# A fused linear attention and gated feed-forward kernel: another written order, full 128-row chunks of k, and a swap of two products

## The chip, the cores and the metric

The kernel runs on one core of one Trainium2 chip. The metric is device time in microseconds (us) of one execution; three runs of the kernel before gave 933.54, 933.70 and 934.96 us, median 933.7 us. The engines are called as the profile calls them: PE (TensorE, the matrix engine), DVE (VectorE), ACT (ScalarE), POOL (GpSimd) and SP (SyncE, which here only issues DMAs).

## The reference

Inputs q, k, v are 8 batches x 8 heads x 576 rows x 64, in float32; the attention output is laid out as x with 4608 tokens x 512 and goes through a gated feed-forward of width 1536.

```
q_s = softmax(q, over the 64 columns);  k_s = softmax(k, over the 576 rows)
kv  = einsum('bhsd,bhse->bhde', k_s, v)
x   = einsum('bhsd,bhde->bhse', q_s, kv)           # -> 4608 x 512
xn  = x / sqrt(mean(x * x, -1) + 1e-6) * rms_g
g   = xn @ w_gate;  val = xn @ w_val
out = (g / (1 + exp(-g)) * val) @ w_out
```

A softmax over the rows of k subtracts each column's maximum, takes the exponential and divides by the sum over the 576 rows; a row with exponential 0 adds nothing to either sum.

## The kernel before

**Tiles and stages.** The 4608 tokens are cut into nine blocks j = 0 to 8 of 512. The 8 heads are four pairs g = 0 to 3. For each batch b and pair g the kernel loads k twice (`kt` by rows, `kd` transposed), takes the column maxima from `kd` (`k_max`, DVE), spreads them over the partitions on PE (`k_rows`), subtracts (`k_sub`), takes exponentials (`k_exp`, ACT) and multiplies with v on PE (`k_mm`, L600). The 576 rows are five chunks: four of 128 and one of 64, two heads each, so `k_mm` is ten matmuls and each stands in the trace as two instructions. For batches 1 to 7 `k_seg` puts the `k_mm` of one pair and the `k_rows` of the next in one bank of PSUM. `kv_hi` and `kv_lo` scale the product and split it into a high and a low word.

**q.** For block j and pair g, `q_load` to `q_mul` make the softmax of q, `q_t` transposes, `q_hi` and `q_lo` split into words, and `q_x` (L796) sums three products on PE for each batch that the block touches: high kv with high q, low kv with high q, high kv with low q. Block 0 and 1 have their own forms (`q_load0` to `q_x0`), and batch 0 transposes k on PE (`k_tr0`).

**Feed-forward.** Weights arrive as 64-bit floats in 36 tiles of 512 KB (`load_w`) in staging slots and are turned into float32 by ACT and DVE or POOL (`conv_low`, `conv_mul`, `conv_one`, `conv_shift`, `conv_sign`). Block 0 uses float32 words (`f1`, L1230; `f2`, L1301), block 1 16-bit words (`f1p`, L1246), blocks 2 to 8 a scheme of seven products per pair of slices instead of eight (`pp`, L1166) with its copies and sums (`ev`), the split of h (`hu_hi`, `hu_lo`) and the output product (`fu`, L1214). `store` scales and writes the output.

**Order.** Nothing is scheduled at build time: the string `ORDER` (some 3,000 steps) is run from first to last, and each engine executes what its steps issue in that order, from its own queue. A suffix `:A`, `:D` or `:P` names the engine (ACT, DVE, POOL) of a step that could run on several. An instruction that waits holds up all that stands behind it on its engine. SP issues all loads and stores in one queue: a load whose tile is still in use holds up every later load.

**Dummy work.** `warm` (L470) multiplies constants before the first product, and `fill` (L476) adds products with zero to an open sum; neither changes a result. `zeros` is the common part:

```
def zeros(t, n, fresh):
    for _ in range(n):
        nc.tensor.matmul(t, lhsT=zero_b..., rhs=ones_b..., start=fresh, stop=fresh)
```

In `ORDER`, `fill.20` is twenty such matmuls at that place. The listing follows with the profile's line numbers.

Of the kernel before, what the change touches and what calls it, by code (L numbers as in the profile page):

```python
# [29 lines left out]
q_exp.0.0 v_load.0.2 q_max0.0.2 q_sum0.0.0 load_w.0.1 q_sub0.0.1:P fill.2 k_mm.0.0 q_exp.0.3 k_rec.0.2 q_sum0.0.3  # L30
kv_norm0.0.0:A q_sub0.0.2:P load_w.1.1 q_exp.0.1 g_abs q_eps0.0.0 q_exp.0.2 q_rec0.0.0 q_sum0.0.1 v_load.0.1
q_mul0.0.0:P conv_low.0.0.1 kd_load.1.0 k_max.0.1 conv_mul.0.0 fill.12 q_t0.0.0 q_eps0.0.3 k_exp.0.1 conv_shift.0.0
load_w.3.0 k_tr0.2.0 conv_sign.0.0 q_c0.0.0:A k_tr0.2.1 k_ev0.2.0:A q_rec0.0.3 fill.2 q_x0.0.0 load_w.2.2 q_eps0.0.1
q_rec0.0.1 q_mul0.0.3:P k_ev0.2.1:A q_sum0.0.2 load_w.1.2 q_mul0.0.1:P conv_low.3.2.1 k_tr0.3.0 x_hi.0.0:D x_sq.0.0
load_w.2.1 x_lo.0.0 k_tr0.3.1 k_ev0.3.0:A k_mm.0.2 q_eps0.0.2 k_ev0.3.1:A q_load0.1.0 q_rec0.0.2 conv_low.0.1.1
k_eps.0.1 k_rec.0.1 q_mul0.0.2:P conv_mul.0.1 k_mm.0.3 k_load.1.0 conv_low.1.0.2 k_eps.0.3 k_rec.0.3 conv_shift.0.1
k_tr0.1.0 v_load.1.0 kv_norm0.0.3:A k_tr0.1.1 conv_sign.0.1 n_sum0.0 v_load.1.1 kv_norm0.0.2:A k_max.1.0 w_hi.0.0.2:P
q_t0.0.3 conv_mul.1.0 q_t0.0.1 q_c0.0.3:D load_w.4.1 conv_low.3.0.2 conv_shift.1.0 q_x0.0.3 q_c0.0.1:A conv_sign.1.0
w_lo.0.0:P f1.0.0.0.0 x_sq.0.3 f1.0.1.0.0 x_hi.0.3:D s_tr k_ev0.1.0:A kd_load.1.1 x_lo.0.3 w_lo.0.1:P k_ev0.1.1:A
fill.3 k_mm.0.1 conv_low.2.2.1 s_top load_w.0.2 conv_low.1.2.1 s_rows s_bits kv_norm0.0.1:A load_w.4.0 k_rows.1.0  # L40
conv_low.2.0.2 q_x0.0.1 k_load.1.1 q_max0.1.0 q_t0.0.2 x_sq.0.1 x_hi.0.1:D q_load0.1.1 q_sub0.1.0:P q_c0.0.2:A
n_sum0.1 x_lo.0.1 q_load0.1.2 v_ones.1.0 q_exp.1.0 q_x0.0.2 k_sub.1.0 k_load.1.2 v_ones.1.1 f1.0.1.0.1 q_sum0.1.0
conv_mul.1.1 f1.0.1.0.3 f1.0.0.0.1 load_w.5.0 f1.0.0.0.3 x_hi.0.2:D x_sq.0.2 k_exp.1.0 conv_shift.1.1 fill.1 n_sum0.2
conv_sign.1.1 f1.0.1.0.2 f1.0.0.0.2 conv_low.0.2.1 f1.0.0.1.0 x_lo.0.2 f1.0.1.1.0 w_hi.1.0.2:P load_w.5.1 f1.0.1.1.1
conv_mul.0.2 f1.0.0.1.1 k_max.1.1 n_sum0.3 conv_low.4.0.2 conv_shift.0.2 kd_load.1.2 f1.0.0.1.2 f1.0.0.1.3 f1.0.1.1.2
conv_sign.0.2 f1.0.0.2.0 f1.0.1.1.3 w_lo.1.1:P f1.0.1.2.0 f1.0.1.2.1 n_t.0 conv_mul.2.0 load_w.4.2 f1.0.1.2.2
f1.0.0.2.1 f1.0.0.2.2 n_y0.0 conv_one.2.0 w_lo.1.0:P f1.1.0 conv_shift.2.0 n_y1.0 conv_mul.2.1 conv_sign.2.0:P
load_w.6.0 conv_low.5.0.2 f1.0.1.2.3 conv_shift.2.1 f1.0.0.2.3 k_mm.1.0 conv_sign.2.1 f1.1.1 v_load.1.2 n_cols.0
w_hi.2.0.2:A load_w.6.1 k_load.1.3 k_max.1.2 conv_low.4.2.1 w_lo.2.0:P q_max0.1.1 kd_load.1.3 conv_mul.1.2 n_rows.0
q_sub0.1.1:P g_mul.0 conv_shift.1.2 f1.2.0 w_lo.2.1:P silu.0 conv_sign.1.2 conv_low.6.0.2 v_ones.1.2 h_mul.0  # L50
load_w.5.2 conv_mul.3.0 q_eps0.1.0 g_mul.1 f1.2.1 conv_shift.3.0 silu.1 conv_sign.3.0 g_mul.2 conv_mul.3.1 load_w.7.0
q_max0.1.2 conv_one.3.1 silu.2 conv_shift.3.1 q_sub0.1.2:P conv_low.5.2.1 q_rec0.1.0 k_rows.1.1 k_eps.1.0 k_rec.1.0
conv_sign.3.1:P h_mul.2 kv_norm0.1.0:A h_mul.1 conv_mul.3.2 w_hi.3.0.2:P load_w.7.1 k_max.1.3 f2.0 conv_shift.3.2
kd_load.2.0 q_exp.1.2 conv_sign.3.2 q_exp.1.1 w_lo.3.0:P k_sub.1.1 load_w.7.2 conv_mul.2.2 q_sum0.1.1 conv_mul.4.0
q_mul0.1.0:P conv_shift.2.2 conv_low.7.0.2 conv_sign.2.2 w_lo.3.1:P q_load0.1.3 k_exp.1.1 conv_shift.4.0 load_w.6.2
conv_mul.4.1 q_eps0.1.1 q_rec0.1.1 conv_mul.4.2 conv_shift.4.1 q_mul0.1.1:P conv_low.7.2.1 f1.3.0 conv_sign.4.1
conv_one.4.0 q_load.2.0 conv_shift.4.2 conv_mul.5.2 conv_sign.4.0:P load_w.8.1 conv_sign.4.2 conv_low.6.2.1
conv_shift.5.2 conv_mul.5.0 load_w.8.2 w_hi.4.0.2:P f2.1 load_w.8.0 o_hi.4:A g_mul.3 conv_shift.5.0 conv_sign.5.0
o_lo.4:P silu.3 conv_sign.5.2 load_w.10.0 conv_mul.5.1 q_max0.1.3 load_w.10.2 fill.20 q_t0.1.0 conv_one.5.1 w_lo.4.1:P
f2.2 conv_shift.5.1 conv_low.8.2.1 q_c0.1.0:D conv_low.8.0.2 q_sub0.1.3:P q_max.2.0 conv_mul.6.0 conv_sign.5.1:P  # L60
q_sum0.1.2 conv_mul.6.1 conv_shift.6.0 conv_one.6.0 w_lo.4.0:P load_w.10.1 f1.3.1 conv_shift.6.1 conv_mul.6.2
conv_low.10.2.1 conv_sign.6.1 conv_sign.6.0:P o_hi.5:A conv_shift.6.2 conv_mul.7.0 o_lo.5:P conv_sign.6.2 f1.4.0
w_hi.5.0.2:A conv_shift.7.0 conv_mul.7.1 conv_sign.7.0 w_lo.5.1:P conv_one.7.1 conv_shift.7.1 load_w.9.0 conv_mul.7.2
w_lo.5.0:P h_mul.3 q_x0.1.0 conv_low.10.0.2 conv_shift.7.2 f1.4.1 conv_sign.7.1:P x_sq.1.0 conv_sign.7.2 x_raw.1.0:A
g_mul.4 load_w.9.2 conv_mul.8.0 load_w.9.1 q_eps0.1.2 q_rec0.1.2 q_half.2.0 conv_mul.8.1 q_mul0.1.2:P f2.3
w_hi.6.0.2:A conv_shift.8.0 q_load.2.1 conv_shift.8.1 conv_mul.8.2 w_lo.6.1:P conv_sign.8.1 silu.4 conv_low.9.2.1
conv_shift.8.2 load_w.11.1 w_lo.6.0:P conv_mul.9.0 h_mul.4 warm.2.13 conv_low.9.0.2 conv_sign.8.2 f1.5.0 h_hi.4:P
q_max.2.1 conv_one.8.0 load_w.11.2 h_lo.4:P conv_shift.9.0 conv_mul.9.1 conv_one.9.1 conv_sign.9.0 conv_sign.8.0:P
f1.6.0 g_mul.5 conv_mul.9.2 conv_shift.9.1 silu.5 load_w.11.0 conv_low.11.2.1 conv_sign.9.1:D conv_mul.10.0
conv_shift.9.2 f2.4 conv_one.10.0 conv_shift.10.0 conv_sign.9.2 conv_mul.10.1 conv_sign.10.0:P g_mul.6 n_sq.0.0  # L70
conv_shift.10.1 k_mm.1.1 o_hi.6:P silu.6 conv_sign.10.1 n_sq.0.1 f1.5.1 v_load.1.3 k_eps.1.1 o_lo.6:P k_rec.1.1
k_load.2.0 kv_norm0.1.1:D conv_mul.11.0 conv_mul.11.1 conv_low.11.0.2 f1.6.1 h_mul.5 w_hi.7.0.2:P conv_one.11.1
conv_shift.11.0 h_hi.5:A conv_shift.11.1 conv_sign.11.0 conv_mul.10.2 w_lo.7.0:P f1.7.0 w_hi.8.0.2:A h_mul.6
conv_shift.10.2 conv_sign.11.1:P conv_mul.11.2 conv_sign.10.2 h_hi.6:A w_lo.8.0:P conv_shift.11.2 k_rows.1.2 k_sub.1.2
w_lo.8.1:P q_exp.1.3 g_mul.7 fill.5 n_col.0.0 k_exp.1.2 n_max.0.0 w_lo.7.1:P f1.7.1 conv_sign.11.2 n_sq.0.2 q_sum0.1.3
v_ones.1.3 h_lo.5:P n_sq.1.0 n_col.0.1 w_hi.9.0.2:A h_lo.6:P k_mm.1.2 n_max.0.1 k_rows.1.3 n_sq.1.1 k_eps.1.2
v_load.2.0 f1.8.0 k_rec.1.2 w_lo.9.1:P k_sub.1.3 k_load.2.1 kv_norm0.1.2:A k_exp.1.3 n_bits.0.1.0 q_eps0.1.3
q_rec0.1.3 w_lo.9.0:P k_mm.1.3 g_mul.8 q_mul0.1.3:P silu.7 q_t0.1.1 k_eps.1.3 k_rec.1.3 f1.8.1 silu.8 q_c0.1.1:D
kv_norm0.1.3:A h_mul.7 n_bits.0.1.1 n_bits.0.1.2 n_bits.0.1.5 w_sc.0.1 n_bits.0.1.3 n_bits.0.1.4 q_x0.1.1 h_mul.8
w_hi.10.0.2:P b_hi.0.2:A n_col.1.0 w_sc.0.0 k_max.2.0 f1.9.0 n_max.1.0 kd_load.2.1 x_sq.1.1 x_raw.1.1:D b_lo.0.2:P  # L80
b_hi.0.3:A b_hi.0.0:A x_acc.1.1:D n_sq.1.2 n_col.1.1 f1.9.1 b_lo.0.0:D v_ones.2.0 k_load.2.2 n_sq.2.2 n_max.1.1
w_lo.10.0:P g_mul.9 n_sq.2.0 b_lo.0.3:D q_t0.1.2 q_max2.2.0 w_lo.10.1:D n_sq.2.1 q_load.2.2 n_col.2.0 f2.5 t_op.0.0:D
silu.9 n_max.2.0 w_hi.11.0.2:P n_sq.3.0 h_mul.9 q_c0.1.2:D b_hi.0.1:A t_hi.0.0:A q_t0.1.3 b_lo.0.1:D n_col.2.1
# [1299 lines left out]
```

## Time and profile before

| | |
|---|---|
| three runs | 933.54, 933.70, 934.96 us |
| the profiled execution | span 930.9 us; the runs' median is 2.8 us above it |
| PE busy | 913.8 us (98%), 6479 matmuls |
| DVE, ACT, POOL busy | 617.3, 559.1, 305.9 us |
| matmuls of L1166 (`pp`) on the chain that ended last | 38% of the span |
| matmuls of L1214 (`fu`) on it | 22% |
| bytes moved | 68.06 MB, 365 GB/s over the first 39 us |

How to read it: the span runs from the first to the last instruction of the program. "Busy" counts time in which at least one instruction of an engine is under way; a matmul's end is modelled, so a wait shorter than its pipeline does not show as idle time. The name `<-` points from what is read to what is written, and "idle before, releaser" names what ended the engine's last wait.

### The profile page before, as it was taken

Reading aid. Unit: us, or ns where it says so; the run is one execution under the profiler, and the core shown is the slowest. Engines: PE = TensorE matmul, PEld = TensorE weight load, DVE = VectorE, ACT = ScalarE, POOL = GpSimd, SP = SyncE. Lnnn points to the kernel's source line nnn. Section 1 sums busy time; section 2 is a strip of 40 time slices with the busy share of each in tenths; the row PEclk is TensorE's granted clock in tenths of the full one; section 3 lists DMA queues with packets and bytes.
Section 4 is the critical chain, followed back from the end, with each engine's and each line's share of the span. In section 5 each row is a group of like instructions: output and inputs, shape, how many; then the busy total and the mean of one; then the engine's idle time right before and its main releaser. Section 6 shows DMA issues by size and latency. Waiting matters only on the chain.

```text
span 930.9 us, 16383 instructions
## 1 busy us (share of the span) xinstructions
PE 913.8 (98%) x6479; PEld 644.0 (69%) x6479; DVE 617.3 (66%) x1330; ACT 559.1 (60%) x880; POOL 305.9 (33%) x304
## 2 busy tenths in 40 slices
...
GB/s 342 360 265 226 61 53 38 36 23 188 54 53 131 33 42 24 110 94 53 66 117 77 65 53 29 36 51 1 38 35 23 1 2 46 1 1 24 23 1 46
DMA packets 29550, 68.06 MB, mean 73 GB/s; under 512 B 3744, under 2 KB 4000, under 8 KB 29472
## 3 DMA queue, kind: packets, MB, share of 16 engines
...
q8 instruction: 51, 0.84, 0.4%
...
## 4 chain that ended last, share of the span: by engine, by line
PE 83%; DVE 6%; ACT 4%; DMA 3%; issue 2%; POOL 1%; SPq 0%; ACTq 0%; POOLq 0%; DVEq 0%
PE ps_gv L1166 38%; PE ps_o L1214 22%; PE ps_o L1301 5%; PE ps_gv L1230 5%; PE ps_gv L1246 4%; PE ps_a L796 2%; PE ps_a L600 2%; DMA qt<-in_q_dram 1%; PE ps_a L560 1%; DMA w_gv<-in_kt_dram 1%; DMA w_br<-in_w_dram 1%; PE ps_a L1021 1%; ACT w_gv L388 0%; PE ps_a L725 0%; DVE x_raw L827 0%
## 5 line engine op out<-in xcount | busy, mean ns | idle before, releaser
L1166 PEld LDWEIGHTS <-w_gv 128*128 128x128 f16 x2016 | 196.0, 98 | 39.7 <-issue 3.2
L1166 PE MATMUL ps_gv<-xo,w_gv 128*128 128x256 f16 x1296 | 155.8, 273 | 0.6 <-ACT w_br L383 0.4
L1166 PE MATMUL ps_gv<-x_op,w_gv 128*128 128x256 f16 x720 | 86.5, 273 | 0.2
L1166 PEld LDWEIGHTS <-w_br 128*128 128x128 f16 x756 | 73.7, 98 | 14.3 <-issue 1.3
L1214 PEld LDWEIGHTS <-hh 128*128 128x128 f16 x504 | 48.9, 98 | 49.8 <-issue 0.4
L1214 PEld LDWEIGHTS <-hl 128*128 128x128 f16 x504 | 49.0, 98 | 47.5 <-issue 0.6
L1214 PE MATMUL ps_o<-w_o,hl 128*128 128x512 f16 x336 | 79.9, 379 | 0.0
L1214 PE MATMUL ps_o<-w_o,hh 128*128 128x512 f16 x336 | 78.4, 379 | 0.0
L1230 PE MATMUL ps_gv<-xo,wf 128*128 128x512 f32 x264 | 66.7, 404 | 0.0
L1166 PE MATMUL ps_gv<-xo,w_br 128*128 128x256 f16 x540 | 66.1, 273 | 0.0
L1230 PEld LDWEIGHTS ps_gv<-xo,wf 128*128 128x128 f32 x264 | 49.0, 188 | 12.9 <-issue 2.8
L1166 PEld LDWEIGHTS <-wf 128*128 128x128 f16 x504 | 49.2, 98 | 8.1 <-issue 0.3
L1181 DVE TENSOR_TENSOR tm<-ps_gv,tm 128x512 f32<-128x512 f32 x29 | 20.0, 689 | 50.9 <-PE ps_gv L1166 47.7
L785 POOL TENSOR_TENSOR ql<-qT,qh 128x512 fp32r<-128x512 f32 x14 | 18.2, 1301 | 87.1 <-ACT qh L383 87.1
L383 ACT COPY ps_gv<-ps_gv 128x512 f32<-128x512 f32 x42 | 24.0, 572 | 36.3 <-PE ps_gv L1166 13.8
L1181 DVE TENSOR_TENSOR w_br<-ps_gv,w_br 128x512 f32<-128x512 f32 x29 | 20.0, 690 | 37.4 <-PE ps_gv L1166 36.8
L1166 PE MATMUL ps_gv<-xo,wf 128*128 128x256 f16 x360 | 43.9, 273 | 0.0
L897 POOL TENSOR_TENSOR acc<-acc,sq 128x512 f32<-128x512 f32 x11 | 14.0, 1270 | 71.8 <-ACT sq L893 71.8
L1246 PE MATMUL ps_gv<-x_op,w_br 128*128 128x512 f16 x144 | 31.9, 379 | 0.0
L383 ACT COPY w_br<-ps_gv 128x512 f32<-128x512 f32 x29 | 17.0, 585 | 23.5 <-PE ps_gv L1166 23.4
L970 POOL TENSOR_TENSOR wf<-w_gv,wf 128x512 fp32r<-128x512 f32 x22 | 28.1, 1293 | 6.7 <-ACT wf L383 6.3
L383 ACT COPY tm<-ps_gv 128x512 f32<-128x512 f32 x29 | 17.0, 585 | 21.5 <-PE ps_gv L1166 21.3
...
## 6 DMA issues: line engine op xcount, KB each, us to landing
...
```

What stands on the lines that cost most here:

```text
L383: (e.copy if e is nc.scalar else e.tensor_copy)(dst, src)
L600: nc.tensor.matmul(ps[h * D:(h + 1) * D, :n1], lhsT=ke[:n, h, j], rhs=vt_[b, g][:n, j, h], start=(j == 0), stop=(j == len(rows) - 1))
L785: on(nc.gpsimd).tensor_tensor(out=ql, in0=qT_[j, g], in1=qh_[j, g][0].bitcast(F32), op=ALU.subtract)
L796: nc.tensor.matmul(px[:, c0:c1], lhsT=wt, rhs=mv[:, c0:c1], start=(i == 0), stop=(i == 2))
L897: on(nc.gpsimd).tensor_tensor(out=acc_[j], in0=acc_[j], in1=sq_[j, g], op=ALU.add)
L970: on(nc.gpsimd).tensor_tensor(out=cut(wl[:, a]), in0=W(s, a), in1=cut(wh[:, a].bitcast(F32)), op=ALU.subtract)
L1166: nc.tensor.matmul(pair(ps, i), lhsT=a[:, wt], rhs=y if i else y.rearrange("p (a c) -> p a c", a=2), start=(first and k == 0 and i == 0 an ...
L1181: nc.vector.tensor_tensor(out=v, in0=bank[j, u, 5 if n == 5 else 3], in1=v, op=ALU.add)
L1214: nc.tensor.matmul(po[2 * n + t], lhsT=a[:, o:o + P], rhs=w, start=(u == 0 and i == 0 and p == 0), stop=(u == NU - 1 and i == 1 and p == 2))
L1230: nc.tensor.matmul(pd[s], lhsT=m[:, a, c * P:(c + 1) * P], rhs=X[j, c][x], start=(n == 1), stop=(n == 3 * NKT))
L1246: nc.tensor.matmul(pd[s], lhsT=w[:, wt], rhs=x, start=(c == 0 and p == 0), stop=(c == NKT - 1 and p == 2))
L1301: nc.tensor.matmul(po[t], lhsT=a[:, t * P:(t + 1) * P], rhs=w, start=(i == 0 and n == 0), stop=(i == NF - 1 and n == len(terms) - 1))
```

## The change

Three things change, and one name follows from them.

- `ORDER` is another sequence of the same steps, with other engines behind many of them; of 53 dummy matmuls of `fill`, 2 are left, and the 37 of `warm` stand elsewhere. Two of its lines:

```
-kd_load.0.0 exp_table constants kd_load.0.3 warm.9 kv_zero0.0 kd_load.0.2 kv_zero.2 q_load0.0.0 kv_zero0.1 q_load0.0.1
+constants warm.2.3 warm.2.12 warm.2.0 warm.2.7 warm.9 warm.2.5 kv_zero0.0 kd_load.0.2 k_max.0.2 k_exp.0.2 kd_load.0.0
```

- In batches 1 to 7 the host fills the last 64 rows of the fifth chunk of k with -1e30 in place of a repeat of the last row, and `k_mm` multiplies all 128 rows of every chunk.

```
-        rows = [min(P, S - c * P) for c in range(C0)]
+        rows = [P if b else min(P, S - c * P) for c in range(C0)]
...
-        "k": pairs(k)[1:, :, :, chunks].transpose(0, 1, 3, 2, 4, 5).reshape(b - 1, g, 128, -1),
+        "k": np.where(past, np.float32(-1e30), pairs(k)[1:, :, :, chunks]).transpose(0, 1, 3, 2, 4, 5).reshape(b - 1, g, 128, -1),
```

- In `q_x` the second and the third product change places.

```
-            for i, (wt, mv) in enumerate(((hi, qh), (lo, qh), (hi, ql))):
+            for i, (wt, mv) in enumerate(((hi, qh), (hi, ql), (lo, qh))):
```

- The output banks are kept under (block, number), `po[j, t]`, since a block's stores may now stand behind the next block's first output product.

Counted over the two instruction lists, PE issues 51 matmuls fewer, all of `fill`; ACT 87 instructions fewer, 12 loads of its function table more than before (76 instead of 64) among them; DVE 30 more and POOL 69 more; the DMAs are the same 204 rows in another order. `ORDER` is one line shorter, so line numbers below it are one less.

**The place where block 0's first `f1` products start, on PE.** Before, from the `k_mm` of batch 0, pair 1 on (L600); x is what `f1` multiplies, `wf` its weights, `tm` the squares for the norm:

```order
L600 MATMUL ps_o<-w_gv 64x64 x10
L994 MATMUL ps_a<-tp,ones 128x1
L560 MATMUL ps_a<-ident,kx 128x128
L725 MATMUL ps_o<-x_raw,ot 128x512
L712 MATMUL ps_o<-ident,x_op_94 128x128 x4
L914 MATMUL ps_a<-tm,mean_w 128x512
L725 MATMUL ps_o<-x_raw,ot 128x512
L1230 MATMUL ps_gv<-xo,wf 128x512 x4
L476 LDWEIGHTS zero_b
L476 MATMUL ps_gv<-ones_b,zero_b 128x512
L914 MATMUL ps_a<-tm,mean_w 128x512
L1230 MATMUL ps_gv<-xo,wf 128x512 x6
```

Now, from the same `k_mm` (L599) on:

```order
L599 MATMUL ps_o<-w_gv 64x64 x10
L724 MATMUL ps_o<-x_raw,ot 128x512 x2
L469 MATMUL ps_gv<-mean_w 128x512 x2
L987 MATMUL ps_a<-ident,mx 1x128
L469 MATMUL ps_gv<-mean_w 128x512 x2
L913 MATMUL ps_a<-tm,mean_w 128x512
L993 MATMUL ps_a<-tp,ones 128x1
L913 MATMUL ps_a<-tm,mean_w 128x512
L559 MATMUL ps_a<-ident,kx 128x128
L1229 MATMUL ps_gv<-xo,wf 128x512 x2
L913 MATMUL ps_a<-sq,mean_w 128x512
L1229 MATMUL ps_gv<-xo,wf 128x512 x15
```

All four transposes of q (L711) and all four `q_x0` (L724) now stand ahead of the first `f1`, where two `f1` products stood between them before; the `fill` is gone.

**The loads of k and v for batch 1, on SP.** `kt` is k by rows, `kd` k transposed, `vt` v, `qt` q; `w_br`, `w_gv` and `w_o` are staging slots of weight tiles. Before:

```order
L518 DMA kt<-in_k_dram 128x640
L680 DMA qt<-in_q_dram 128x512 x2
L518 DMA kt<-in_k_dram 128x640
L425 DMA w_br<-in_w_dram 128x1024 x2
L526 DMA kd<-in_kt_dram 128x576
L425 DMA w_br<-in_w_dram 128x1024
L425 DMA w_gv<-in_w_dram 128x1024
L541 DMA vt<-in_v_dram 128x650
L425 DMA w_gv<-in_w_dram 128x1024
L518 DMA kt<-in_k_dram 128x640
```

Now, with the last eight weight tiles:

```order
L424 DMA w_br<-in_w_dram 128x1024
L424 DMA w_gv<-in_w_dram 128x1024 x2
L424 DMA w_o<-in_w_dram 128x1024
L424 DMA w_br<-in_w_dram 128x1024 x2
L517 DMA kt<-in_k_dram 128x640
L424 DMA w_br<-in_w_dram 128x1024
L517 DMA kt<-in_k_dram 128x640
L424 DMA w_br<-in_w_dram 128x1024
L517 DMA kt<-in_k_dram 128x640
```

The rows of k for pairs 2 and 3 of batch 1 stood behind 14 and 19 of the 36 weight tiles, and now stand behind 36 and 34 of them (the last and the first `kt` of the second piece; the one between is of batch 2).

**One `q_x`, on PE.** Block 3, pair 0; `kv_hi_108` and `kv_lo_109` are the two words of kv of one batch, `kv` those of the other, `qh` and `ql` the words of q. Before:

```order
L796 MATMUL ps_a<-qh,kv_hi_108 128x256
L796 MATMUL ps_a<-qh,kv_lo_109 128x256
L796 MATMUL ps_a<-ql,kv_hi_108 128x256
L796 MATMUL ps_a<-qh,kv 128x320 x2
L796 MATMUL ps_a<-ql,kv 128x320
```

Now, the same `q_x`:

```order
L795 MATMUL ps_a<-qh,kv_hi_108 128x256
L795 MATMUL ps_a<-ql,kv_hi_108 128x256
L795 MATMUL ps_a<-qh,kv_lo_109 128x256
L795 MATMUL ps_a<-qh,kv 128x320
L795 MATMUL ps_a<-ql,kv 128x320
L795 MATMUL ps_a<-qh,kv 128x320
```

The number of products is the same; the one with `ql` stands one place earlier.

## Rows read from the trace of the kernel before

**Rows 1.** Page, part 1: engine, busy us (share of the span), instructions.

```profile
PE 913.8 (98%) x6479; PEld 644.0 (69%) x6479; DVE 617.3 (66%) x1330; ACT 559.1 (60%) x880; POOL 305.9 (33%) x304
```

**Rows 2.** Windows: stretch in us, its length, busy us (instructions) per engine.

```profile
core 0: us, PE busy (x) PEld busy (x) DVE busy (x) ACT busy (x) POOL busy (x), PEclk, DMA share, GB/s
0.00:12.00 12.00, 10.57 (x42) 8.61 (x42) 5.39 (x13) 5.09 (x10) 4.89 (x22) 1.00 0.83 281
12.00:39.00 27.00, 22.82 (x163) 13.47 (x162) 21.67 (x48) 22.47 (x43) 12.77 (x15) 1.00 1.03 402
39.00:112.00 73.00, 71.58 (x339) 50.01 (x338) 61.05 (x121) 62.95 (x94) 48.12 (x46) 1.00 0.58 196
112.00:176.00 64.00, 62.55 (x321) 45.86 (x320) 47.14 (x110) 52.35 (x78) 35.15 (x34) 1.00 0.15 48
176.00:265.00 89.00, 88.16 (x515) 44.23 (x514) 64.02 (x155) 66.56 (x109) 59.70 (x57) 1.00 0.28 89
265.00:931.00 666.00, 658.16 (x5107) 481.79 (x5105) 418.00 (x886) 349.72 (x551) 145.22 (x136) 1.00 0.14 43
```

**Rows 3.** Windows, of line L476 (fill) alone.

```profile
0.00:39.00 39.00, 5.19 (x20) 1.79 (x20) 1.00 0.97 365
39.00:112.00 73.00, 5.76 (x25) 2.44 (x25) 1.00 0.58 196
112.00:176.00 64.00, 2.23 (x8) 0.78 (x8) 1.00 0.15 48
```

**Rows 4.** Windows, of line L470 (warm) alone.

```profile
0.00:39.00 39.00, 10.12 (x35) 7.91 (x35) 1.00 0.97 365
```

**Rows 5.** Groups by form, L600: count, busy us, mean ns, idle before.

```profile
L600 PE MATMUL ps_a<-vt,kt 128*64 128x65 f32 x448 | 19.2, 228 | 1.1 <-ACT kt L573 0.6 <-POOL hh L383 0.6
L600 PE MATMUL ps_a<-vt,kt 64*64 64x65 f32 x112 | 9.3, 243 | 0.0
```

**Rows 6.** Timeline of PE: start us, length us, line, count; one k_mm.

```profile
45.17 0.95 PE L600 MATMUL ps_a<-vt,kt 128*64 128x65 f32 x20
46.05 0.50 PE L1230 MATMUL ps_o<-xo,wf 128*128 128x512 f32 x1
```

**Rows 7.** Timeline of PE, block 0's first products and a wait.

```profile
25.53 1.03 PE L1230 MATMUL ps_gv<-xo,wf 128*128 128x512 f32 x2
...
28.42 0.95 PE L600 MATMUL ps_o<-w_gv 128*64 128x64 f32 x20 [1.10 <-ACT w_gv L383]
...
39.19 2.87 PE L1230 MATMUL ps_gv<-xo,wf 128*128 128x512 f32 x10
```

**Rows 8.** Timeline of ACT ahead of that wait.

```profile
25.49 1.15 ACT L439 ACTIVATE w_gv<-w_gv 128x1024 int32<-128x1024 uint32 x1 [0.74 <-DMA w_gv<-in_w_dram]
...
27.63 0.74 ACT L383 COPY w_gv<-ps_o 128x512 f32<-128x512 f32 x2
```

**Rows 9.** Timeline of PE, three products of one q_x.

```profile
301.38 0.36 PE L796 MATMUL ps_a<-qh,kv_hi 128*128 128x256 f32 x1
301.58 0.28 PE L796 MATMUL ps_a<-qh,kv_lo 128*128 128x256 f32 x1
301.70 0.28 PE L796 MATMUL ps_a<-ql,kv_hi 128*128 128x256 f32 x1
```

**Rows 10.** Waits of SP's queue, weight tiles: total us, times, longest.

```profile
SPq L425 <- DVE w_gv L464: 15.7, 6, 6.2
SPq L425 <- POOL w_gv L461: 11.0, 4, 2.9
SPq L425 <- DVE w_o L464: 9.9, 8, 2.4
```

**Rows 11.** Groups of ACT by form: one of its table loads.

```profile
L752 ACT ACT_TABLE_LOAD x16 | 20.5, 1283 | 1.7 <-DVE qt L748 1.4
```

More of the change, by code (lines that the diff above doesn't have):

```diff
@@ L30 @@
[L30 to L83, printed above, removed]
-h_hi.7:A v_load.2.1 f2.6 n_max.2.1 w_lo.11.0:P n_sq.3.1 o_hi.7:A q_max.2.2 h_lo.7:P q_x0.1.2 o_lo.7:D h_hi.8:A
@@ new lines @@
+k_ev0.3.1:A v_load.0.1 warm.2.10 conv_mul.0.0 k_mm.0.0 conv_low.0.0.1 conv_shift.0.0 warm.2.13 conv_sign.0.0
+kv_norm0.0.0:A q_eps0.0.1 k_load.1.0 q_rec0.0.1 q_mul0.0.1:D k_exp.0.1 k_eps.0.1 load_w.1.1 kd_load.1.0 q_mul0.0.0:P
+q_load0.1.0 q_t0.0.0 q_c0.0.0:A load_w.2.0 fill.1 k_tr0.1.0 q_exp.0.3 k_ev0.1.0:A q_sum0.0.3 q_x0.0.0 x_sq.0.0
+load_w.2.1 load_w.1.2 q_load0.1.1 g_abs q_sub0.0.2:P q_exp.0.2 q_eps0.0.3 q_rec0.0.3 q_mul0.0.3:P q_sum0.0.2
+q_eps0.0.2 x_hi.0.0:A k_mm.0.2 kv_norm0.0.2:A k_mm.0.3 k_rec.0.3 conv_mul.0.1 q_rec0.0.2 conv_low.0.1.1 k_rec.0.1
@@ new lines @@
+q_t0.0.1 q_c0.0.1:D load_w.3.2 kv_norm0.0.3:D n_sum0.0 q_t0.0.3 q_mul0.0.2:P k_tr0.1.1 q_t0.0.2 warm.2.11 q_c0.0.3:A
+conv_shift.0.1 conv_sign.0.1 x_lo.0.0 q_c0.0.2:A load_w.0.2 load_w.3.1 k_max.1.0 q_x0.0.3 w_hi.0.0.2:P w_lo.0.0:P
+k_ev0.1.1:A k_mm.0.1 kv_norm0.0.1:D q_x0.0.2 q_x0.0.1 conv_low.1.0.2 conv_mul.1.0 conv_shift.1.0 conv_sign.1.0
+x_hi.0.3:A q_max0.1.0 kd_load.1.1 warm.2.1 x_hi.0.2:A x_lo.0.3 s_tr s_top warm.2.2 x_lo.0.2 x_sq.0.1 kv_zero.3
+q_load0.1.2 q_sub0.1.0:P n_sum0.1 s_rows s_bits x_sq.0.2 n_sum0.2 load_w.3.0 k_rows.1.0 k_sub.1.0 f1.0.1.0.0 x_sq.0.3
@@ new lines @@
+kv_hi.2.0:A q_sub.2.2:D q_half.2.3 q_max2.2.3 kv_lo.2.0 q_sub.2.3:D kv_hi.2.1:D q_t.2.1 t_lo.1.0:P kv_lo.2.1 h_lo.16:D
+f2.15 v_ones.2.2 k_seg.3 q_exp.2.2 o2_hi.10 q_sum.2.2 q_half2.2.2 f1p.19.0 silu1.19 q_sum2.2.2 q_rec.2.2 k_eps.2.2
+k_rec.2.2 t_op.1.2:P t_hi.1.1:P o2_lo.8 q_x.2.0 kv_hi.2.2:D kv_lo.2.2 kd_load.3.2 v_load.3.0 x_sq.2.0 k_max.3.2
+t_op.1.3:P k_sub.2.3 f2.16 k_load.3.1 x_raw.2.0:A k_load.3.0 o2_lo.10 q_hi.2.1:P q_lo.2.1:D h_lo.17:P f2.17 v_ones.3.0
+h_hi.18:A q_load.3.0 q_mul.2.2:D o2_hi.11 q_t.2.2 q_exp.2.3 kd_load.3.3 q_sum.2.3 k_exp.2.3 q_half2.2.3 q_sum2.2.3
@@ new lines @@
+t_op.3.2:P t_op.2.3:P k_seg.4 k_sub.3.0 k_exp.3.0 q_rec.2.3 q_x.2.1 x_sq.2.1 h_lo.18:P f2.18 q_hi.2.2:P q_max.3.0
+q_half.3.0 q_max2.3.0 q_lo.2.2:P q_load.3.1 q_max.3.1 v_load.3.1 k_max.3.3 q_sub.3.0:P t_lo.1.1:D k_eps.2.3 k_rec.2.3
+kv_hi.2.3:D kv_lo.2.3 f1p.19.1 q_mul.2.3:P q_t.2.3 x_raw.2.1:A v_ones.3.1 t_hi.1.2:A q_x.2.2 q_hi.2.3:A k_seg.5
+k_eps.3.0 x_raw.2.2:A h_mul1.19 t_lo.1.2:P k_sub.3.1 q_lo.2.3:D x_acc.2.1:P q_half.3.1 q_load.3.2 k_rec.3.0
+kv_hi.3.0:D x_sq.2.2 q_exp.3.0 h_hi.19:P kd_load.4.0 q_sum.3.0 q_half2.3.0 x_acc.2.2:P f1p.20.0 silu1.20 kv_lo.3.0
@@ new lines @@
+ev.3.1.2 k_seg.11 k_eps.4.2 k_rec.4.2 k_sub.4.3 pp.3.1.7 ev.3.1.3 q_t.4.3 q_max.5.1 pp.3.1.5 ev.3.1.5 pp.3.1.4
+hu_lo.3.0.1:D fu.3.0.1.0 ev.3.1.9 x_sq.4.1 store.2.1 pp.3.1.3 kv_hi.4.2:A kv_lo.4.2 ev.3.1.11 hu_hi.3.1.1 pp.3.2.1
+fu.3.0.1.1 ev.3.1.6 hu_hi.3.0.0 hu_lo.3.0.0:D ev.3.1.10 store.2.3 ev.3.2.0 pp.3.2.6 q_load.5.2 k_exp.4.3 q_half2.5.0
+ev.3.2.2 fu.3.0.0.0 q_half.5.1 k_load.5.2 q_max2.5.1 q_sub.5.1:P pp.3.2.2 ev.3.2.8 q_max.5.2 q_half.5.2 hu_lo.3.1.1:P
+fu.3.1.1.0 q_x.4.2 q_exp.5.1 pp.3.2.7 q_max2.5.2 q_sub.5.2:P q_exp.5.2 q_sum2.5.0 v_load.5.2 q_rec.5.0 q_mul.5.0:P
```

486 lines of the change are left out of this document (258 added, 228 removed).

## The prediction

> **What bounds the kernel now.** I read the busy shares first: PE is busy for 913.8 of 930.9 us, and DVE and ACT for 617.3 and 559.1 [rows 1]. So PE's own instruction stream is the path, and the reader should ask of each edit only two things: how much PE time it removes, and whether PE then waits. Next come the windows by stage [rows 2]. In the first 39 us PE is busy for 33.4 (10.57 + 22.82), but DVE (27.1) and ACT (27.6) are nearly as full and the DMA share is 0.83 and 1.03: a stage limited by how data, conversions and small steps follow each other. From 39 to 265 us PE is idle for 1.42, 1.45 and 0.84 us. From 265 on, it is busy for 658.16 of 666 us: 7.84 us idle in 5,107 instructions. The granted clock is 1.00 in every stretch. Third, the windows of the two dummy lines: `fill` takes 5.19, 5.76 and 2.23 us, 13.2 in all and all of it before 176 us [rows 3], and `warm` 10.12 us before 39 [rows 4]. Dummy time is idle time under another name: it says where the next real product was not ready. Counted so, the first 39 us hold 33.4 - 5.2 - 10.1 = 18.1 us of real PE work, 39 to 112 us hold 1.42 + 5.76 = 7.2 us without any, and 112 to 265 hold 1.45 + 2.23 + 0.84 = 4.5.
>
> Durations come from one profiled execution; my sum is made against its span of 930.9 us, and the runs' median is 2.8 us above that, which I add at the end.
>
> **Full chunks of k.** The two sizes of `k_mm` matmul have rows of their own: 19.2 us over 448 with 128 rows, 43 ns each, and 9.3 us over 112 with 64 rows, 83 ns each [rows 5]. That a smaller tile should cost twice as much looks odd, but the timeline agrees: a whole `k_mm` of 20 instructions starts at 45.17 and the next product at 46.05 [rows 6], 0.88 us, and 16 x 43 + 4 x 83 ns make 1.02 by busy time, which overlaps. The count of instructions stays. If the 112 take 43 ns like the others, 112 x 40 ns = 4.5 us of PE time go, 0.16 per `k_mm`, in 28 `k_mm`. Most lie in a stretch where PE is 98.8% busy, so I take the whole 4.5 us as gain, in the last stage. Ends: the idle time of that stage may vanish besides (-4.5 - 7.84 = -12.3) or double (+3.3), since all its instructions have new neighbours. I stay at -4.5, because the order shows both signs: of the 42 units of `pp`, 24 now have two or more other product groups between the sixth and seventh products, where 8 had before (more time for the copies and sums between); but 10 have just one `k_seg` or `q_x` between the first and the sixth, where 1 had. The -1e30 rows reach ACT, DVE and the DMAs in tiles of the old shapes: nothing.
>
> **The swap in `q_x`.** In the row of one `q_x` the products start at 301.38, 301.58 and 301.70 [rows 9]; no instruction is added or removed. The product with `ql` is wanted one place, about 0.12 us, earlier; when `ql` is late, that is a wait of 0.12 us. With four pairs in each of blocks 1 to 8 that is at most 32 x 0.12 = 3.8 us, and if two products with the same `kv_hi` beside each other spared as much, -3.8. I take 0: in this row PE waits for neither, and the ends lie inside those of the last stage.
>
> **Order, first 39 us.** The steady `f1` products begin at 39.19; the first two came at 25.53 already, and between them PE took the last transposes, `q_x0`, squares and a `k_mm` which waited 1.10 us for an ACT copy [rows 7]. That copy stood at 27.63 behind a weight conversion started at 25.49, which had itself waited 0.74 for a DMA [rows 8]. The new order puts all transposes and all `q_x0` ahead of the first `f1`, drops the fill, moves casts of weights from ACT to POOL, and spreads most `warm` into the first ten us. The lower end: DVE's 27.1 us of work must be done anyway, so 39 - 27 = -12. The upper end: another pair of such waits of 1.10, +2. I take the middle of what can be saved, -6: the 5.19 of fill and a little of the 5.6 idle, because the DMA share of 1.03 says loads cannot come sooner.
>
> **Order, 39 to 112 us.** 7.2 us hold no real work, so the ends are -7.2 and 0, and I take -4: ACT's 62.95 and DVE's 61.05 of 73 us leave too little slack to close it all, and POOL, which takes most of the moved casts, has 48.12. **112 to 265 us:** ends -4.5 and 0, I take -2.5.
>
> Twelve more table loads on ACT: one is 1283 ns [rows 11], so 12 are 15.4 us on an engine that is busy for 60%. As the last stage has ACT at 349.72 of 666 us, I price them at nothing there, and they are part of why I do not close the early gaps fully. [...]
>
> **The sum.** -6 - 4 - 2.5 - 4.5 = -17: span 930.9 - 17 = 913.9, and with 2.8 around it 916.7, so 917 us. For a wait put in the place of a gap one checks what stands behind it: PE is one queue, so each wait for a late tile delays every later product by its full length.
>
> **Rivals.**
>
> *The gaps come back as waits (15%).* Fill may have been only a cover: without it PE waits as long for the same `x`, weights or h. Then only `k_mm` pays: 930.9 - 4.5 = 926.4, about 929 us. For it speaks that ACT and DVE are at 84 to 86% from 39 to 112; against it that they issue in another order too.
>
> *Nearly all gaps close (13%).* Three quarters of each lower end: 0.75 x (12 + 7.2 + 4.5 + 12.3) = 27, span 903.9, 907 us. The saturated last stage speaks against it: 7.84 us in 5,107 instructions are tiny waits.
>
> *Slower: SP's queue holds up batch 1 (10%).* The rows of k for pairs 2 and 3 of batch 1 stood behind 14 and 19 weight tiles and now behind 36 and 34. A weight tile's load waits on SP for its staging slot; those waits sum to 15.7, 11.0 and 9.9 us, the longest 6.2 [rows 10], and every load behind waits with it. PE would reach the `k_mm` of these pairs and stand still, with the `f1` and `f2` of block 0 and later block 1 behind it. Three further long waits carried to PE, each with the steps from loaded k to exponential as late as the copy above, 3 x (6.2 + 1.1) = 22 us, against my -17 give span 936, about 939 us. It decides from 17 us of such waits. Against it: the steps that wait for these rows move back in the order too, and the DMA share of 0.58 from 39 us on leaves room.
>
> *Clock (3%).* Without fill, PE's early gaps are real ones. [...]
>
> *No net effect (4%):* the four stages lose what `k_mm` gains, about 934 us.
>
> **Chances and range.** Forecast 55%, with 909 to 925 as its own range (half of the order's -12.5 less or more, and 2 for the last stage). A difference of up to 0.2%, 1.9 us, is about what a measurement of this kernel cannot tell from no change. Faster by more than that: 55 + 15 + 13 = 83%, and a part of the last two cases, 84%; within it 6%; slower 10%. The range of 8 in 10 reaches from 903 (all but the best of the second rival) to 931 (with the first rival inside): 903 to 931 us.
>
> **What the new profile would show.** *k:* one form of `k_mm` in batches 1 to 7, near 43 ns per matmul, a whole one 0.72 us. Wrong if the 64-row form's time went to the others. *Early order:* steady `f1` at about 33 us, `pp` beginning at about 252 instead of 265. *Fill:* two matmuls of it, with no new waits of over 1 us at `f1` or `k_mm`; the first rival shows such waits instead, on PE, and the third rival names `kt` or an exponential of batch 1 as releaser, with SP's wait for a staging slot before it. *Last stage:* about 662 us long, 8 of them idle. *Clock:* 1.00 everywhere; any lower value before 39 us is the fourth rival. What would make me wrong most easily is a last stage whose small waits change by several us, since I have no row that prices its new neighbours.

## The result, and the profile after

The changed kernel takes 946.3 us (943.6 to 947.4, four runs) where the kernel before takes 934.1: a ratio of 1.013 with a 95% interval of 1.0112 to 1.0147. It is slower by 12 us where 17 us less were forecast. The profiled spans differ by 14.1 us (945.0 against 930.9), and the question is where.

The page's first part, of the kernel after:

```profile
PE 908.5 (96%) x6428; PEld 638.0 (68%) x6428; DVE 644.4 (68%) x1360; ACT 523.6 (55%) x793; POOL 361.7 (38%) x373
```

Against [rows 1] PE is busy for only 5 us less, ACT for 35 less, DVE for 27 more and POOL for 56 more. Fixed windows no longer compare like with like, so I cut both kernels at the same products: the start of the steady `f1` (after, two `f1` products early), the first `f1p` (block 1), the first `pp` (block 2). Columns as in [rows 2]. Before:

```profile
0.00:39.20 39.20, 33.59 (x205) 22.11 (x205) 27.25 (x61) 27.71 (x53) 17.86 (x36) 1.00 0.97 365
39.20:161.30 122.10, 120.68 (x598) 88.84 (x597) 98.44 (x210) 100.55 (x148) 76.27 (x72) 1.00 0.41 139
161.30:264.50 103.20, 100.91 (x573) 50.78 (x571) 73.07 (x176) 80.66 (x129) 66.00 (x63) 1.00 0.25 80
264.50:931.00 666.50, 658.66 (x5111) 482.24 (x5109) 418.50 (x886) 350.22 (x552) 145.72 (x136) 1.00 0.14 43
```

After:

```profile
0.00:33.30 33.30, 30.27 (x186) 20.58 (x187) 24.25 (x59) 22.22 (x43) 12.65 (x24) 1.00 0.96 362
33.30:151.90 118.60, 114.41 (x561) 84.13 (x560) 107.98 (x213) 108.13 (x159) 85.39 (x89) 1.00 0.44 157
151.90:271.00 119.10, 106.32 (x597) 52.97 (x596) 107.75 (x229) 68.46 (x95) 55.40 (x58) 0.96 0.25 77
271.00:945.00 674.00, 657.53 (x5089) 480.34 (x5087) 404.38 (x862) 324.83 (x496) 208.27 (x203) 1.00 0.13 42
```

Call what lies ahead of the first `f1p` stage A, from there to the first `pp` stage B, the rest stage C. A shrinks from 161.3 to 151.9 (-9.4); B grows from 103.2 to 119.1 (+15.9); C from 666.5 to 674.0 (+7.5). The row of B tells where to look: DVE, busy for 73.07 of 103.2 us before, is busy for 107.75 of 119.1, 53 instructions more (in C it has 24 fewer), while ACT and POOL have less to do there than before. PE has one `k_seg` and four small products more in B; its idle time there goes from 2.3 to 12.8 us and its busy time from 100.91 to 106.32. The granted clock, 1.00 in all of the kernel before, is 0.96.

PE's waits in stage B (engine, line waited for, total us, times, longest), where the longest of before was 1.4:

```profile
PE ps_a L599 <- DVE kv_lo L650: 7.6, 2, 4.9
PE ps_gv L1245 <- ACT tm L1251: 2.2, 3, 0.8
```

`k_seg` takes a bank of PSUM that `kv_lo` of an earlier pair must first have read; there are two such banks. The timeline of PE at that wait (start us, length us, idle time before in brackets):

```profile
207.00 2.75 PE L1300 MATMUL ps_o<-oh,hl 128*128 128x512 f16 x12
214.66 1.35 PE L599 MATMUL ps_a<-vt,kt 128*64 128x65 f32 x20 [4.91 <-DVE kv_lo L650]
...
216.54 3.88 PE L1245 MATMUL ps_gv<-x_op,w_br 128*128 128x512 f16 x12
```

And the timeline of DVE ahead of it:

```profile
200.49 0.75 DVE L547 TENSOR_REDUCE kx<-kd 128x1 f32<-128x576 f32 x1 [2.46 <-DMA kd<-in_kt_dram]
201.16 0.68 DVE L730 TENSOR_REDUCE st<-qt 128x16 f32<-128x512 f32 x1
...
205.51 1.29 DVE L644 TENSOR_TENSOR kv<-ot,kv 128x128 fp32r<-128x128 f32 x1
...
211.43 0.69 DVE L1131 TENSOR_TENSOR w_gv<-w_gv 128x512 f32<-128x512 f32 x1
212.04 0.28 DVE L644 TENSOR_TENSOR kv<-ot,kv 128x128 fp32r<-128x128 f32 x1
...
213.83 0.57 DVE L650 SCALAR_TENSOR_TENSOR kv_lo<-ps_a,rs,kv_hi 64x64 fp32r<-64x64 f32 x2
```

Just ahead of this DVE stood still for 2.46 us, for a load of `kd` that took 5.1 us; SP issued it at 195.34, as soon as the `k_max` before it had ended. From 200.49 to 213.83 DVE does not pause once: softmax steps of q for later blocks (L730, L755, L769, L747) and sums of weights (L1129, L1131) stand in its queue ahead of `kv_lo`. Nor are its operations all as short as before: the same L644 takes 0.28 us at 212.04 and 1.29 at 205.51. The row of POOL at that time:

```profile
204.93 1.71 POOL L1131 TENSOR_TENSOR w_gv<-w_gv 128x512 f32<-128x512 f32 x1
```

POOL's operation ends at 206.64, DVE's at 206.80. This is the pattern of every stretched operation (over 0.3 us longer than the first quartile of its form): all 70 in the kernel after, and all 40 before, overlap a POOL operation that began first. They sum to 55.5 us of extra time after and 27.8 before; in stage B 15 with 13.7 us and 8 with 6.5. Of the 70, 62 have two inputs (`TENSOR_TENSOR`, `SCALAR_TENSOR_TENSOR`) and 8 have one; 163 reductions (one input) that overlap a POOL operation in the kernel after are not stretched. The prediction did not weigh this.

The long wait has a second price. Windows of 5 us around it (columns as above; the granted clock stands behind POOL's busy time):

```profile
204.00:209.00 5.00, 5.00 (x25) 2.29 (x24) 4.97 (x11) 1.49 (x3) 2.58 (x3) 1.00 0.00 0
209.00:214.00 5.00, 0.75 (x4) 0.14 (x2) 4.86 (x14) 3.79 (x7) 0.00 (x0) 0.80 0.01 2
214.00:219.00 5.00, 4.34 (x29) 2.68 (x30) 4.71 (x14) 0.33 (x1) 0.00 (x0) 0.52 0.37 120
219.00:224.00 5.00, 5.00 (x27) 2.70 (x26) 4.71 (x13) 3.50 (x6) 2.58 (x4) 1.00 0.44 151
```

PE, idle for some 5 us, comes back with a granted clock of 0.52, and twelve products of `f1p` take 3.88 us at 216.54 where they take 2.75 at 231.83, with a granted clock of 1.00: 1.1 us more. The second wait for `kv_lo` is shorter, and the twelve products behind it cost 1.7 us more, with a granted clock of 0.59 from 239.0 to 243.2 us:

```profile
238.13 0.80 PE L599 MATMUL ps_a<-vt,kt 128*64 128x65 f32 x20 [2.67 <-DVE kv_lo L650]
...
239.18 4.44 PE L1245 MATMUL ps_gv<-x_op,wf 128*128 128x512 f16 x12
```

In all of B this price is 4.4 us: PE is busy for 106.32 us, and for the same products in `pool_light` below, at a clock of 1.00, for 101.97. So B's 15.9 us are some 10.5 of waiting, 4.4 of slow clock and 1 of added products.

### The profile page after: what moved, and what is told of

Its sections match the earlier page's. It is cut to its first block, busy times and chain, and to the rows that moved or that the text cites. A ratio compares the mean times of both kernels' runs of the same rounds, so it can differ in the third digit from the quotient of the medians.

```text
span 945.0 us, 16314 instructions
## 1 busy us (share of the span) xinstructions
PE 908.5 (96%) x6428; PEld 638.0 (68%) x6428; DVE 644.4 (68%) x1360; ACT 523.6 (55%) x793; POOL 361.7 (38%) x373
## 4 chain that ended last, share of the span: by engine, by line
PE 66%; DVE 23%; ACT 5%; issue 4%; DMA 1%; POOL 1%; ACTq 0%; SPq 0%; DVEq 0%; POOLq 0%
PE ps_gv L1165 34%; PE ps_o L1213 17%; PE ps_gv L1229 3%; PE ps_o L1300 2%; PE ps_gv L1245 2%; PE ps_a L795 2%; PE ps_a L599 1%; DVE sw L736 1%; DVE kx L547 1%; DVE kt L564 1%; PE ps_gv L469 1%; DMA qt<-in_q_dram 1%; DVE xo L882 1%; DVE ps_a L455 1%; DVE x_raw L826 1%
## 5 line engine op out<-in xcount | busy, mean ns | idle before, releaser
L896 POOL TENSOR_TENSOR acc<-acc,sq 128x512 f32<-128x512 f32 x15 | 20.5, 1364 | 68.7 <-ACT sq L892 68.7
L1180 DVE TENSOR_TENSOR wf<-ps_gv,wf 128x512 f32<-128x512 f32 x17 | 11.6, 685 | 36.5 <-PE ps_gv L1165 36.4
L599 PE MATMUL ps_a<-vt,kt 128*64 128x65 f32 x560 | 23.0, 230 | 10.4 <-DVE kv_lo L650 7.6
L599 PEld LDWEIGHTS ps_a<-vt,kt 128*64 128x64 f32 x560 | 19.2, 140 | 19.0 <-issue 11.0
```

The lines of the kernel that those rows point to most:

```text
L599: nc.tensor.matmul(ps[h * D:(h + 1) * D, :n1], lhsT=ke[:n, h, j], rhs=vt_[b, g][:n, j, h], start=(j == 0), stop=(j == len(rows) - 1))
L896: on(nc.gpsimd).tensor_tensor(out=acc_[j], in0=acc_[j], in1=sq_[j, g], op=ALU.add)
L1180: nc.vector.tensor_tensor(out=v, in0=bank[j, u, 5 if n == 5 else 3], in1=v, op=ALU.add)
```

## The experiments

Each kernel was timed in three rounds beside the kernel before; ratios are to it. A, B and C are the stages' lengths in the profiled execution of each. The kernels with `light` in their names leave out part of the work.

| kernel | median us | ratio (95%) | A | B | C |
|---|---|---|---|---|---|
| before | 934 | 1 | 161.3 | 103.2 | 666.4 |
| after | 946.3 | 1.0130 (1.0112 to 1.0147) | 151.9 | 119.0 | 674.0 |
| order_alone | 1031.2 | 1.1038 (1.1022 to 1.1055) | 182.6 | 124.9 | 719.0 |
| engines_alone | 961.8 | 1.0299 (1.0283 to 1.0314) | 169.2 | 108.9 | 683.3 |
| k_and_q_alone | 931.9 | 0.9979 (0.9966 to 0.9993) | 161.4 | 103.3 | 663.9 |
| early_part_alone | 922.5 | 0.9879 (0.9864 to 0.9893) | 152.3 | 104.6 | 663.6 |
| dve_light | 935.3 | 1.0014 (1.0003 to 1.0024) | 150.5 | 109.4 | 672.8 |
| pool_light | 935.2 | 1.0014 (1.0003 to 1.0025) | 151.7 | 107.1 | 675.6 |
| new_order_to_first_pp | 935.9 | 1.0020 (1.0008 to 1.0032) | 152.2 | 115.5 | 664.7 |
| new_order_from_first_pp | 955.8 | 1.0233 (1.0215 to 1.0250) | 160.9 | 104.8 | 686.4 |
| casts_on_act_late | 959.1 | 1.0260 (1.0237 to 1.0283) | 151.7 | 118.4 | 688.4 |
| no_fill | 931.6 | 0.9975 (0.9962 to 0.9988) | 164.1 | 102.9 | 663.4 |
| cut_at_f1p_14 | 926.7 | 0.9925 (0.9910 to 0.9940) | 150.4 | 110.7 | 663.5 |
| cut_at_f1p_18 | 926.0 | 0.9915 (0.9900 to 0.9930) | 152.1 | 108.9 | 663.4 |
| dve_light_late | 939.1 | 1.0050 (1.0032 to 1.0068) | 151.8 | 118.7 | 667.9 |
| pool_light_late | 940.6 | 1.0062 (1.0040 to 1.0085) | 151.1 | 118.3 | 670.1 |
| pool_light_late_control | 919.8 | 0.9845 (0.9830 to 0.9861) | 152.0 | 106.0 | 661.1 |
| cut_at_f1_9 | 925.7 | 0.9907 (0.9893 to 0.9922) | 158.3 | 102.7 | 663.7 |

**Order or engines?** In `order_alone` the new order keeps the engines of before; two of the 353 steps that go back, each to its old suffix:

```
-kv_hi.2.1:D
+kv_hi.2.1:A
...
-o_x_hi.3.4:P
+o_x_hi.3.4:A
```

> The changed kernel with every step back on the engine it had before; the new order of steps, the full chunks of k and the swap in q_x stay. Theory Q (the order itself puts too much DVE work ahead of kv_lo between the first f1p and the first pp, so DVE's queue sets that stage): 940 to 948 us, PE waits of several us for kv_lo remain, DVE busy for over 85% from 165 to 262 us. Theory E (71 casts moved from ACT to POOL stretch DVE's two-input operations, 25 us before, 50 us after): 922 to 930 us, and DVE's stretched operations back at about 40. Both in part: 932 to 939.

It took 1031 us, outside all three ranges. `engines_alone` is the converse (the suffixes of the new order in the order of before).

> The order of before (with its fill), every step on the engine that the changed kernel gives it, and the edits of k and q_x. Theory Q: about 930 us, 934 less the 4.1 of k_mm. Theory E: 938 to 946 us, with over 60 stretched DVE operations and PE waits before the first pp.

It took 962, slower than either theory had it. Here the written order and its engines can't be priced apart: either without the other is slower than the two together. As a test of the theories both are inconclusive: the steps then stand where the queues of other engines had put them.

**The edits of k and q.** The diff is the one shown ahead of the prediction without the lines of `ORDER`.

> The kernel before with only the full chunks of k, the swap in q_x and the new keys of the output banks. Theories Q and E both: 28 x 0.147 us = 4.1 us less than before, about 930 us, k_mm at 0.73 us. Theory S (the swap or the full rows themselves cost something: later waits for ql, or a longer k_exp): 934 us or more.

The result lies between: 2.0 us less (0.7 to 3.2). `k_mm` fell from 0.88 to 0.73 us in the trace. The 18 of 28 that lie in stage C are worth 18 x 0.147 = 2.6, and C fell by 2.5; A and B, with the other ten, did not move. That PE waits for others there anyway is likely, and not shown.

**Where the order gains and where it loses.** Six kernels take the new order and its engines up to a step (five) or from it on; what has not run by then follows in the other order (the edit in short):

```
-ORDER = new
+ORDER = new[: first f1p] + [s for s in old if s not in new[: first f1p]]
```

> The new order, engines included, up to the first f1p; all steps that are left then in the order and on the engines of before; k and q_x as changed. Theory Q and theory E: the 9.3 us that the first f1p comes earlier are kept, with 4.1 for k_mm: 921 us (918 to 924). Rival D (the early stage is only shorter because work of the next stage was put off): the gain is lost before the first pp, 928 to 932 us.

922.5 us: the early gain is real and is kept; the best of all kernels with the full result. The rival D falls.

> The new order and engines up to the first pp, what is left in the order and on the engines of before, k and q_x as changed. If the last stage's own order costs time (674.0 us against 666.5 before, and 4 us of k_mm not seen): 934 to 939. If it is only late for the backlog that the stage ahead leaves: 943 to 947.

With the new order up to the first `pp` the time is 935.9: B is long (115.5), C as short as in the order of before (664.7). So the loss of some 10 us in C (674.0) comes with C's own order, not from a backlog that B leaves.

> The order and engines of before (with its fill) up to the first pp, and what is left in the new order on the new engines, k and q_x as changed. If the last stage's own order costs time: 936 to 941 us, with waits of PE for DVE from 265 us on. If the backlog does: 928 to 932.

955.8, more than expected. Its C is 686.4, 12.4 more than in the kernel after; 10.1 of these are one wait right behind the change of order, likely because the new order then starts from a state that it wasn't made for. This longest wait of PE ends at 279 us, at one of block 1's `f2` behind the change of order (columns as in the waits above):

```profile
PE ps_o L1301 <- DVE hl L1282: 10.1, 1, 10.1
```

> New order and engines up to the products of slice 14 of block 1's first products (about 165 us), the rest as before. Where the lead still grows there: 919 to 922 us. If DVE's backlog has begun by then: 924 to 930.

> The same with the cut at slice 18 (about 190 us, ahead of PE's first long wait for kv_lo). Theory Q (the work that fills DVE behind 200 us is queued by the new order ahead of the cut already): 926 to 934. If only the order behind the cut makes the wait: 919 to 923.

They took 926.7 and 926.0: already a few slices of `f1p` in the new order cost B 4 to 6 us over `early_part_alone`, though PE's first long wait for `kv_lo` lies behind both cuts. The times lie in the ranges of theory Q (the second at its edge), but they do not show its mechanism: PE's longest waits in B are 3.2 us for ACT and 2.4 for DVE with the cut at 14, 3.0 for ACT and 1.7 for POOL with the cut at 18, and none of note for `kv_lo`. The change of order may itself cost this much.

> New order and engines up to the first f1 of slice 9 (about 112 us), the rest as before. If the whole early gain is made by then: 920 to 923 us; if the order from 112 to 152 us adds to it: 924 to 928.

925.7, with A at 158.3, but A's length misleads here. The second half of slice 8, the last `f1` ahead of the cut, starts at 105.3 us, in the kernel after at 105.0, in the kernel before at 115.2: the early gain is made by then. (One `k_mm` and three transposes, somewhat over 1 us, stand behind that point now.) Behind the cut the old order gives some 7 us back: PE waits 2.3 us for DVE, and the next twelve `f1` products take 4.84 us instead of 2.98 (the mean granted clock of this run is 0.998). A cut has a price of its own.

**What makes B long.** The edit, with `thin` true from the first `f1p` to the first `pp` for the named steps:

```
+    def cols(a):                      # an eighth of the last dimension
...
+        return Thin(e) if thin[0] and e is nc.vector else e
...
+            tensor_reduce(out=st, in_=cols(qt_[j, g]) if thin[0] else qt_[j, g], ...
```

> The changed kernel, but from the first f1p to the first pp the steps t_op, x_nrm, x_acc, q_sub, q_mul that stand on DVE, and the reductions k_max, q_max, q_sum, work on an eighth of their columns only (so the rest of these tiles keeps its old values). That takes 38 x 0.5 = 19 us from DVE in that stage, where it is busy for 107.8 of 119.1 us. Theory Q (DVE's queue sets this stage): PE's waits for kv_lo of 7.6 us go, the first pp starts at 256 to 262 us instead of 271.0, and the whole takes 932 to 938. Rival L (the stage is late for loads or for ACT, DVE only follows): 943 to 947.

935.3: B 109.4 instead of 119.0. The waits for `kv_lo` there fell from 7.6 to 2.8 us. Theory Q's range held; rival L falls as the main cause, though DVE still waits 3.3 us for the load of `kd`.

`pool_light` has `nc.gpsimd` in place of `nc.vector`, and the reductions whole.

> The same cut, but of the 16 of these steps that stand on POOL in that stage, DVE's stay whole. Theory P (DVE's two-input operations stand still while a POOL operation runs; 8 of the 16 stretched DVE operations of the stage overlap these): 8 x 1 us of DVE go, pp starts at 262 to 266, 937 to 942 us. Theory M (the moved operations alone fill DVE, the stretching lies beside other waits): 944 to 947.

935.2, better than expected. The window of its stage B:

```profile
151.70:258.70 107.00, 101.97 (x596) 51.51 (x594) 97.16 (x229) 68.07 (x95) 39.48 (x58) 1.00 0.28 85
```

DVE does as many instructions as in the kernel after (229), of full size, and is busy for 10.6 us less, since POOL's shorter ones hold it up less: its stretched operations in B fall from 15 with 13.7 us to 6 with 3.6. The longest wait of PE is down to 2.1 us and the granted clock stays at 1.00, so the price of the clock is gone too. That is 11.9 us of the 15.9. Both theories are parts of one: DVE's queue is full, by moved work and by standing beside POOL; taking 11 to 13 us from it in either way gives back 10 to 12.

**What makes C long.**

> The changed kernel, but the 47 casts to a high word that it moved from ACT to POOL behind the first pp are on ACT again. Theory C (these casts cost the last stage its 10 us: 674.0 us from the first pp to the end, where the order of before needs 664): 936 to 941 us. Rival O (the new order of that stage fits the new engines and no others; casts on ACT now stand behind its copies and table loads): 946 to 960.

The diff sets 47 suffixes, as `-o_x_hi.3.4:P` and `+o_x_hi.3.4:A`. 959 us, with C at 688.4: ACT is no better place for these casts in this order, and PE's longest waits in C now name ACT (6.4 and 4.2 us). Theory C's time did not come; but as with `order_alone` the steps then stand where other queues had put them, so this does not show that the casts cost nothing.

> The changed kernel, but from the first pp on the reductions k_max, q_max and q_sum read an eighth of their columns only: 55 x 0.5 = 27 us less on DVE in that stage, where it is busy for 404 of 674 us. Theory V (in the last stage too PE waits because DVE's queue runs late): the stage takes 662 to 669 us, the whole 934 to 941. Rival O (the 10 us lie in the order of PE's own products and in waits for ACT): 943 to 947.

939.1, C 667.9: 6 of the 10 us, and PE's waits for DVE in C fall from 7.9 to 3.0 us. The edit is that of `dve_light` from the first `pp` on, for the three reductions.

> The changed kernel, but from the first pp on the 30 steps x_acc, q_sub, x_nrm and t_op that stand on POOL work on an eighth of their columns only. Theory V in its form with POOL (DVE stands still beside POOL: 40 stretched operations of 30.8 us in that stage against 28 of 18.8 in the order of before): up to 10 us less, 935 to 942. Rival O: 943 to 947.

> early_part_alone with the same cut of the POOL steps from the first pp on. Its last stage takes 663.6 us with PE idle for 7; theory V: at most 3 us less, 919 to 923, so that what pool_light_late gains is of the new order. If it gains as much as pool_light_late, the cut speeds any order and says nothing on this one.

940.6 with C 670.1, 3.9 us less than after; the control's C is 2.5 less than that of `early_part_alone`. So the standstill beside POOL explains only some 1.4 of C's 10 us (3 by the medians of the whole); DVE's queue at most some 6 (whether the lighter DVE would speed the order of before as well was not tried); the rest stays open. Of the waits of PE in C that the profile lists, 11.8 us, DVE is named for 7.9 and ACT for 3.6:

```profile
PE ps_a L795 <- DVE kv_lo L650: 2.1, 2, 1.8
PE ps_gv L1165 <- DVE w_br L1180: 1.7, 3, 0.8
PE ps_gv L1165 <- DVE tm L1180: 1.7, 2, 1.4
PE ps_gv L1165 <- ACT ps_gv L382: 1.2, 1, 1.2
```

**What fill was for.** All `fill` steps are taken from `k_and_q_alone`:

> The kernel before with the edits of k and q, and without its 53 dummy products of fill; nothing else moves. Theory F (fill is cover: what it fills is a wait for something else, so PE waits instead): 929 to 934 us, as with the k edit alone. Theory G (fill takes PE's time from real work): 918 to 925. If the granted clock falls for the gaps: above 934.

931.6 against 931.9 with it. Its windows of the first 39 us and of 39 to 112 [rows 2]:

```profile
0.00:39.00 39.00, 29.80 (x181) 20.68 (x182) 26.51 (x60) 27.13 (x53) 17.00 (x36) 0.96 0.97 359
39.00:112.00 73.00, 65.90 (x284) 46.48 (x283) 60.26 (x119) 60.64 (x90) 46.15 (x43) 0.95 0.58 199
```

PE is busy for less, waits instead, and its clock falls to 0.96 and 0.95. A is 2.7 us longer than with it in the profiled execution; the medians do not differ. Theory F holds, `fill` covered waits; the fall of the clock came as the third case had it, its time above 934 did not.

## Why the prediction was wrong

The step that failed is "112 to 265 us: ends -4.5 and 0, I take -2.5": B came out 15.9 us longer, and the part of A behind slice 8 as long as before. I bounded what the new order could do by PE's own idle and dummy time, so that a stage could only get shorter. DVE's 30 more instructions, counted over the whole kernel, got no term in the sum. Stage by stage the count was there to be read from the two orders: between the first `f1p` and the first `pp` DVE's instructions go from 175 to 232, 11 of them `kv_hi` taken from ACT, others sums and low words taken from POOL or moved up from behind the first `pp`. At the 73.07 us for 176 in the row of before, 0.42 each, 57 more are 24 us; with the 7 that it stands longer beside POOL that is nearly the 34.7 measured. With 73 + 24 = 97 us of DVE in a stage forecast at some 100, 0 was no upper end. PE then waits for `kv_lo` in DVE's queue, 7.6 us, and pays 4.4 more in clock. The last stage failed second, by its upper end.

- **First 39 us, -6: right in size.** The thirteenth `f1` product, which begins the steady run at 39.19 before [rows 7], starts at 33.79. It is the order that gains it; the prediction put most of it down to the 5.19 us of fill, which `no_fill` shows to be cover.
- **39 to 112 us, -4: right.** At the second half of slice 8 of `f1` the kernel after is 10.2 us ahead, some 9 without the work that it has put off by then; 5.4 of these are the first 39 us. A as a whole is 9.4 us shorter, and `early_part_alone` keeps it.
- **Full chunks, -4.5: mechanism right, size off.** 0.147 per `k_mm` measured where 0.16 was forecast, but only the 18 in stage C show: 2.0 us, where the prediction took all 28 into the last stage.

The group of `k_mm` after has one form, 23.0 us / 560 = 41 ns each, as [rows 5] have for the 128-row matmuls:

```profile
L599 PE MATMUL ps_a<-vt,kt 128*64 128x65 f32 x560 | 23.0, 230 | 10.4 <-DVE kv_lo L650 7.6 <-ACT kt L572 2.1 <-issue 0.6
```

- **The swap, 0: not tested alone.** No run tells it from the edit of k; together they gain 2.0.
- **Last stage otherwise unchanged: wrong.** Its own order costs 9 us (674.0 against 664.7 with the order of before behind the same first part). The upper end, PE's idle time there doubled, was passed: 7.84 us became 16.5.
- **Rival "gaps come back as waits":** true of the order of before without fill, not of the new one, whose first part fills the gaps with work.
- **Twelve more table loads, nothing:** no run tests it; ACT is busy for 35 us less than before.
- **Rival of SP's queue:** right in sign, wrong in mechanism. Single waits of SP for staging slots are longer than in [rows 10], though with 6.7 for POOL they sum to about as much (36.4 against 36.6):

```profile
SPq L424 <- DVE w_o L463: 17.7, 5, 9.7
SPq L424 <- DVE w_gv L463: 12.0, 2, 8.3
```

but the waits of PE in stage A stay below 1 us each, apart from the 1.4 for the first constant that the kernel before has too, and its waits for the exponential of k sum to 0.7. The rows of k come in time.
- **Rival of the clock:** not at the start, where it was placed (1.00 throughout A), but behind the 4.91 us wait in B (0.52); `no_fill` shows it in A (0.96 and 0.95). The 3% were the author's estimate: in the kernel before, the granted clock is 1.00 throughout.
